# Second head's keys loaded by quarters, x tiles 10 and 11 loaded later, half of a tile's statistics moved: a fused LayerNorm, attention and gated FFN kernel

## The chip, the core and the metric

The kernel runs on one core of a Trainium2 chip. The core has a matrix engine (TensorE, PE in the profile, with its weight loads listed as PEld), a vector engine (DVE), a scalar engine (ACT), GpSimd (POOL) and a sync engine (SP) that does nothing here but issue DMAs. The metric is the device time of one execution in microseconds.

## The reference

```python
xn = layernorm(x)                                   # x: 2048 x 640, bf16
q  = (xn @ wq) as 32 heads of 192
s  = softmax(q @ k_cache.T * 192**-0.5) @ v_cache   # 2048 keys per head, not causal
s  = s.reshape(2048, 32 * 192) @ wo
h  = silu(xn @ w1) * (xn @ w3)                      # F = 1536
g  = silu(h @ w2)
out = x + s * g
```

Keys and values come from a cache, so only the queries are projected here. Rows of x are normalised over their 640 columns, without scale or bias.

## The kernel before

The 2048 rows of x are 16 tiles of 128 rows, and four tiles make a block of 512 queries. Each of the 32 heads is worked in four passes, one for each block. A pass has eight steps p = 0 to 7. Step p takes the two key tiles p and p + 8 (128 keys each): `scores` (L506) makes six matmuls into one of the two buffers of tile `st2`, `weights` (L513) takes the exponential on ACT and writes `pT2`, and `values` (L546) makes 16 matmuls that add to the two output banks `obank0` and `obank1`. The value matmuls run about a step behind the scores. At the end of a pass `evict` (L522) reads each bank on DVE into `osum`, and the next pass can write a bank only when it has been read.

A head of 192 columns doesn't fit 128 partitions, so the keys, turned by the DMA, lie in three tiles: `KA` has columns 0 to 127 of all 2048 keys, `KB` columns 64 to 191, and `KC` is put together from them by POOL (L154, L155), for the first two heads in two halves. `KC` copy 0 takes keys 1024 to 1535 of `KA` and keys 0 to 511 of `KB`; copy 1 takes keys 1536 to 2047 and 512 to 1023. Steps 0 to 3 of a pass therefore read keys 0 to 511 and 1024 to 1535, and steps 4 to 7 the others.

From the third head on everything is loaded far ahead. The first two heads are different: there the program starts, and x has to be loaded, normalised and turned while the first passes are running already. The passes of the first two heads are interleaved as in `order` (head, block): (0, 0), (1, 0), (0, 1), (0, 2) and so on; they are numbered n = 0, 1, 2, ... The rest is written out by hand. `posts` names what is put behind step p of pass n, and `extras` what is put into it. Nearly all of these calls are pinned, so each engine runs them in the order in which the program calls them:

- `load_x(engine, t0, t1)` (L194) loads tiles t0 to t1 - 1 of x.
- `ln_stats(i)` makes the statistics of tile i on DVE: two `bn_stats` of 320 columns and one `bn_aggr` (L237, L238).
- `ln_root(i0, n)` makes 1 / sqrt(var + eps) of n tiles on ACT, a logarithm (L244) and an exponential (L247).
- `scale_and_turn(i)` normalises tile i on DVE (L255, tile `xn`) and turns it into `xnT` with a DMA from SP (L266).
- `late_project(h, qb)` projects the queries of a block (L348). In pass 1, step 5 it does head 0, block 1, which reads the turned tiles 4 and 5 in the first half of its matmuls, and 6 and 7 in the second.
- `next_bound` (L443, L446, L449) makes the bound that stands for the row maximum in the exponentials of a pass. For pass 1 it needs `KC` copy 0 of head 1 (`first_key_maxima`, L415 and L424).

SP's queue is run in program order as well. Ahead of the change it holds, after the keys of the first head: values 0 (first half), x tiles 4 and 5, `KA` of head 1, values 0 (second half), `KB` of head 1, x tiles 6 and 7, values 1 (first half), x tiles 8 and 9, values 1 (second half), x tiles 10 and 11, then the turned tiles 4 to 7, x tiles 12 to 15, and the turned tiles 8 to 11. In the program as built, each of these DMAs also waits for the DMA eight places ahead of it to have landed, since eight semaphores are used in turn.

After the 32 heads come the output projection, the FFN's second product and the stores (L865, L889). They aren't touched.

Of the kernel before, what the change touches and what calls it, by code (L numbers as in the profile page):

```python
# [11 lines left out]
BF16 = mybir.dt.bfloat16  # L12
F32 = mybir.dt.float32
I32 = mybir.dt.int32

P = 128
# [14 lines left out]
def _kernel_impl(ctx, tc, A_x, A_k_cache, A_v_cache, A_wq, A_wo, B_w1, B_w3, B_w2, out):  # L31
    nc = tc.nc
    _, SQ, D = A_x.shape
    _, H, SK, dh = A_k_cache.shape
# [8 lines left out]
    HALF = SK // 2  # L43
# [22 lines left out]
    pin = tc.keep_in_program_order  # L66
# [31 lines left out]
    kvp = kvstack.enter_context(tc.tile_pool(name="kvp", bufs=3))  # L98
# [23 lines left out]
    def load_key_part(h, s, half, k0, k1, keep):  # L122
        d0 = (0, DH - P)[s]
        return keep(nc.sync.dma_start_transpose(out=half[:, k0:k1], in_=A_k_cache[0, h][k0:k1, d0:d0 + P]))  # L124

    def load_key_half(h, s, keep):
        half = kvp.tile([P, SK], BF16, tag=("KA", "KB")[s], name=("KA", "KB")[s])
        load_key_part(h, s, half, 0, SK, keep)
        return half
# [9 lines left out]
    def load_values_part(h, vt, r0, r1):  # L139
        of = A_v_cache[0, h].rearrange("(t r p) d -> p t r d", t=2, p=P)  # L140
        to = vt[:].rearrange("p (t r) d -> p t r d", t=2)
        for t in range(2):
            pin(nc.sync.dma_start(out=to[:, t, r0:r1, 0:DH], in_=of[:, t, r0:r1, :]))  # L143
# [33 lines left out]
    with ExitStack() as actx:  # L177
# [6 lines left out]
        lnp = lctx.enter_context(tc.tile_pool(name="lnp", bufs=2, side="right"))  # L184
# [4 lines left out]
        nsub = 2  # L189
        mv = lnx.tile([P, NQT, nc.vector.BN_AGGR_DIM], F32, name="mv")  # L190
        x_all = lnx.tile([P, NQT, D], BF16, name="x_all")

        def load_x(eng, t0, t1):
            pin(eng.dma_start(out=x_all[:, t0:t1, :], in_=x2[t0 * P:t1 * P, :].rearrange("(t p) d -> p t d", p=P)))  # L194
# [35 lines left out]
                                      reason="not all at once")  # L230
                    behind = None

        def ln_stats(i):
            st6 = lnp.tile([P, nsub, nc.vector.BN_STATS_DIM], F32, tag="st6", name="st6")
            xr = x_all[:, i, :].rearrange("p (a f) -> p a f", a=nsub)
            for a in range(nsub):
                pin(nc.vector.bn_stats(out=st6[:, a, :], in_=xr[:, a, :]))  # L237
            return pin(nc.vector.bn_aggr(out=mv[:, i, :], in_=st6[:]))  # L238

        rstd = {}  # L240

# [45 lines left out]
        squares = stats_on_scalar(1)  # L287
        squares()
        keys0 = second_keys(ln_stats(0))
        values0 = kvp.tile([P, NKT, DH + 2], BF16, tag="vt", name="vt")  # L290
        load_values_part(0, values0, 0, 4)
        load_x(nc.sync, 4, 6)
        KA1 = load_key_half(1, 0, pin)
        load_values_part(0, values0, 4, 8)
        keys1 = KA1, load_key_half(1, 1, pin)
        load_x(nc.sync, 6, 8)
        values1 = kvp.tile([P, NKT, DH + 2], BF16, tag="vt", name="vt")
        load_values_part(1, values1, 0, 4)
        load_x(nc.sync, 8, 10)
        load_values_part(1, values1, 4, 8)  # L300
        load_x(nc.sync, 10, 12)

        keep_busy(2, behind=ln_stats(2))
        ln_root(0)
        keep_busy(1, behind=ln_stats(3))
        ln_root(2)
        for i in range(4):
            ln_scale(i)
        turned = []
        for i in range(4):  # L310
            pool, tag = (ps_st, "st2") if i < 2 else (ps_o, f"ob{3 - i}")
# [360 lines left out]
        for h in range(2):  # L672
# [14 lines left out]
        }  # L687
        posts = {
            (0, 0): ((complete_second,),),
            (0, 2): ((ln_root, 4), (scale_and_turn, 4), (scale_and_turn, 5), (first_key_maxima, 1)),  # L690
            (0, 3): ((next_bound, 1, 0), (lambda: loads.pop("second half")(),)),
            (0, 5): ((ln_stats, 6), (ln_stats, 7)),
            (1, 0): ((ln_root, 6),),
            (1, 1): ((scale_and_turn, 6), (scale_and_turn, 7), (load_x, nc.sync, 12, 16)),
            (1, 2): ((ln_stats, 8), (ln_stats, 9)),
            (1, 3): ((ln_stats, 10), (ln_stats, 11)),
            (1, 5): ((scale_and_turn, 8), (scale_and_turn, 9), (scale_and_turn, 10), (scale_and_turn, 11)),
            (2, 2): ((ln_stats, 12), (ln_stats, 13)),
# [340 lines left out]
@with_exitstack  # L1039
def kernel(  # L1040
    ctx: ExitStack,
    tc: tile.TileContext,
    A_x: bass.AP,
    A_k_cache: bass.AP,
    A_v_cache: bass.AP,
    A_wq: bass.AP,
    A_wo: bass.AP,
    B_x: bass.AP,
    B_w1: bass.AP,
    B_w3: bass.AP,  # L1050
    B_w2: bass.AP,
    out: bass.AP,
):
    _kernel_impl(ctx, tc, A_x, A_k_cache, A_v_cache, A_wq, A_wo, B_w1, B_w3, B_w2, out)
# [30 lines left out]
```

## Time and profile before

| what | us |
|---|---|
| median of 3 runs | 1936.01 |
| lowest and highest of them | 1935.34, 1936.47 |
| the profiled execution | 1934.81 |
| its span, first to last instruction | 1933.0 |
| PE busy in the span | 1926.7 |
| ACT busy | 1278.1 |
| DVE busy | 1029.6 |
| POOL busy | 414.5 |

All times of rows below count from the start of the span. A row of the timeline gives start, duration, engine, line of the kernel, operation, output and input, and how many instructions of the kind are merged into it; in square brackets stands the idle time of the engine ahead of it and who ended it. "SPq" is SP's queue: the duration is that of issuing, and the landing of the data is told in another view, counted from the start of issuing. The granted clock of TensorE was 1.000 in the whole span.

### The profile page before, as it was taken

What the parts mean: (1) busy time and instruction counts of PE and PEld (TensorE: products, weight loads), DVE (VectorE), ACT (ScalarE), POOL (GpSimd) and SP (SyncE); (2) the same over time, 40 slices, a digit from 0 to 9 for tenths busy, and PEclk for the clock granted to TensorE, in tenths of its full rate; (3) what the DMA queues carried; (4) which work ended last, traced back from release to release, by engine and by line L of the source; (5) the groups of instructions that cost most, each with busy time, mean ns of one, the idle gap of its engine ahead of it and who ended that gap; (6) DMA issues with size and microseconds to landing.
All of it is one profiled execution on the core that took longest, in us unless ns stands there. A gap on an engine that the chain in (4) does not pass through costs nothing.

```text
span 1933.0 us, 60455 instructions
## 1 busy us (share of the span) xinstructions
PE 1926.7 (100%) x27269; PEld 1411.1 (73%) x27269; DVE 1029.6 (53%) x1892; ACT 1278.1 (66%) x1296; POOL 414.5 (21%) x637
## 2 busy tenths in 40 slices
PE   9999999999999999999999999999999999999999
PEld 6789899998777766666666666666666666577776
DVE  7775555565656565656565555555565554521111
ACT  7777777777777777777777777777777777210000
POOL 2432222222222222222222222222222110000000
PEclk9999999999999999999999999999999999999999
DMA  8532323232213232233432232323232102937873
GB/s 181 105 77 55 77 47 85 47 85 43 65 45 68 51 68 57 63 82 77 109 63 69 55 77 55 76 47 85 47 85 45 36 8 76 281 67 137 156 153 57
DMA packets 361672, 152.84 MB, mean 79 GB/s; under 512 B 312544, under 2 KB 355232, under 8 KB 361408
## 3 DMA queue, kind: packets, MB, share of 16 engines
q1 hardware_dynamic: 346832, 120.12, 29.5%
q0 software_dynamic: 7872, 23.60, 4.7%
q10 hardware_dynamic: 6704, 5.21, 1.0%
q8 instruction: 214, 3.51, 0.7%
q14 instruction: 50, 0.41, 0.1%
HBM read 56.23 MB, written 31.98 MB: 46 GB/s over the span
## 4 chain that ended last, share of the span: by engine, by line
PE 98%; DVE 1%; SPq 1%; DMA 0%; issue 0%; ACT 0%
PE st L506 35%; PE obank L546 34%; PE ps L348 14%; PE ps_s L865 11%; PE ps_f L889 3%; PE ps_gu L332 1%; PE ps_gu L348 0%; SPq L124 0%; DMA x_all<-in_A_x_dram 0%; DVE osum L522 0%; DVE st L237 0%; SPq L143 0%; DVE st L415 0%; DVE pa L487 0%; DVE ostage L529 0%; DVE qF L393 0%
## 5 line engine op out<-in xcount | busy, mean ns | idle before, releaser
L513 ACT ACTIVATE pT<-st,nb 128x1024 bf16<-128x1024 f32 x960 | 1068.4, 1113 | 326.6 <-PE st L506 322.2
L546 PEld LDWEIGHTS <-pT 64*128 64x128 bf16 x16384 | 754.3, 94 | 201.4 <-issue 1.7
L546 PE MATMUL obank<-vt,pT 64*128 64x193 bf16 x16384 | 872.7, 243 | 0.4 <-DVE osum L522 0.4
L522 DVE TENSOR_REDUCE osum<-obank 128x386 f32<-128x772 f32 x256 | 234.2, 956 | 580.2 <-PE obank L546 580.1
L506 PE MATMUL st<-qA,KA 64*128 64x512 bf16 x2048 | 409.8, 376 | 0.1
L506 PE MATMUL st<-qS,KB 64*128 64x512 bf16 x1024 | 385.1, 376 | 0.0
L506 PE MATMUL st<-qS,KC 64*128 64x512 bf16 x1024 | 384.9, 376 | 0.0
L506 PE MATMUL st<-qD,KC 64*128 64x512 bf16 x960 | 361.2, 376 | 0.0
L506 PE MATMUL st<-qF,KB 64*128 64x512 bf16 x960 | 361.0, 376 | 0.0
L348 PE MATMUL ps<-xnT,w 64*128 64x512 bf16 (+1 forms) x2540 | 318.7, 374 | 0.0
L382 POOL COPY qS<-qA 64x512 bf16<-64x512 bf16 x254 | 161.7, 637 | 616.3 <-ACT qA L392 609.2
L506 PEld LDWEIGHTS <-KC 64*128 64x128 bf16 x2048 | 192.4, 94 | 99.8
L348 PEld LDWEIGHTS <-w 64*128 64x128 bf16 x2540 | 146.7, 94 | 96.9
L865 PE MATMUL ps_s<-wo_sb,oT 128*128 128x320 bf16 (+2 forms) x1536 | 208.8, 299 | 0.0
L506 PEld LDWEIGHTS <-KB 64*128 64x128 bf16 x2048 | 192.4, 94 | 5.5
L865 PEld LDWEIGHTS <-oT 128*128 128x128 bf16 x1536 | 148.2, 98 | 60.6
L529 DVE TENSOR_TENSOR ostage<-osum,rl_all 128x384 bf16<-128x384 f32 x256 | 155.4, 607 | 8.8
L506 PEld LDWEIGHTS <-KA 64*128 64x128 bf16 x2048 | 127.4, 93 | 15.4 <-issue 1.4
L108 POOL DMA_DIRECT2D w<-in_A_wq_dram x60 | 52.9, 882 | 289.1 <-PE ps L348 288.9
L393 DVE CAST qF<-ps 128x512 bf16<-128x512 f32 x120 | 82.9, 690 | 52.2 <-ACT qA L392 52.2
L870 DVE SCALAR_TENSOR_TENSOR tmp<-ps_s,g_all 128x320 f32<-128x320 f32 (+2 forms) x32 | 15.6, 487 | 176.1 <-PE ps_s L865 176.1
L376 DVE TENSOR_REDUCE st<-qA 128x1 f32<-128x512 bf16 (+1 forms) x130 | 87.3, 672 | 4.2 <-ACT qA L392 4.1
(101 smaller groups left out, 1131.4 us busy)
## 6 DMA issues: line engine op xcount, KB each, us to landing
o_scr<-ostage SPq DMA_DIRECT2D x64, 384.0 KB, 2.7
vt<-in_A_v_cache_dram SPq DMA_DIRECT2D x30, 768.0 KB, 6.1
wo_sb<-in_A_wo_dram POOLq DMA_DIRECT2D x1, 7680.0 KB, 32.6
w<-in_A_wq_dram POOLq DMA_DIRECT2D x30, 160.0 KB, 3.4
hT_scr<-hblk SPq DMA_DIRECT2D x16, 256.0 KB, 3.0
xt<-in_A_x_dram POOLq DMA_DIRECT2D x16, 160.0 KB, 8.7
w<-in_B_w_dram POOLq DMA_DIRECT2D x30, 80.0 KB, 2.6
w<-in_A_wq_dram POOLq DMA_DIRECT2D x30, 80.0 KB, 2.8
```

Of the source, the lines that this page charges most:

```text
L108: return lambda eng: keep(eng.dma_start(out=w[:, :, c0:c1], in_=src[:, s0:s0 + c1 - c0].rearrange("(c p) d -> p c d", p=P)))
L348: mm = pin(nc.tensor.matmul(out[:, t * 512 + t0 * P:t * 512 + (t0 + step) * P], lhsT=ws[t][ROWS[r], c, :], rhs=rows_of(qb, c, ROWS[r], t0, ...
L376: pin(nc.vector.tensor_reduce(out=hd["st"][r, 2 + s, qb:qb + 1], in_=src[r, qb * 512:qb * 512 + n], axis=AX.X, op=ALU.max, apply_absolute_ ...
L382: return [lambda t=t: keep(copy(out=hd["qS"][ROWS[t], qs], in_=hd["qA"][ROWS[1 - t], qs])) for t in range(2)]
L393: pin(cast(out=hd["qF"][:, qs], in_=ps[:, 512:1024]))
L506: pin(nc.tensor.matmul(st2[:, t * 512:(t + 1) * 512], lhsT=keys, rhs=q[ROWS[t], qs], start=(s == 0), stop=(s == 2)))
L513: pin(nc.scalar.activation(out=pT2[:, c0:c1], in_=st2[:, c0:c1], func=ACT.Exp, scale=SCALE, bias=nb))
L522: pin(nc.vector.tensor_reduce(out=osum[:], in_=ob[:].rearrange("p t (j c) -> p j c t", j=2)[:, :, 0:DH + 1, :], axis=AX.X, op=ALU.add))
L529: pin(nc.vector.tensor_tensor(out=ostage[:, b * 2:b * 2 + 2, hg * DH:(hg + 1) * DH], in0=osum[:, :, 0:DH], in1=rl.unsqueeze(2).to_broadcas ...
L546: pin(nc.tensor.matmul(acc["o"][b][:, r, j * 256:j * 256 + DH + 1], lhsT=pT2[ROWS[r], t * 512 + i * P:t * 512 + (i + 1) * P], rhs=vt[ROWS[ ...
L865: pin(nc.tensor.matmul(ps, lhsT=oT[:, k, :], rhs=wo_sb[:, k, c0:c1], start=(k == 0), stop=(k == OC - 1)))
L889: pin(nc.tensor.matmul(ps[:, pi * 512:pi * 512 + c1 - c0], lhsT=hT[:, fc, qsl], rhs=w2_sb[:, fc, c0:c1], start=(fc == 0), stop=(fc == FC - ...
```

## The change

The two transposing loads of the second head's keys, of 2048 keys each, become eight of 512 keys. The four for steps 0 to 3 stand where `KA` and `KB` were loaded; the four for steps 4 to 7 stand behind the load of x tiles 8 and 9 and ahead of the second half of values 1. The load of x tiles 10 and 11 goes from the end of that list to behind the turning of tiles 4 and 5. `ln_stats` can do one half of a tile: the second `bn_stats` of tile 7 and its `bn_aggr` go from pass 0, step 5, to pass 1, step 1, which lies behind the evictions of pass 0 on DVE. `ln_root(6)` goes from behind step 0 of pass 1 to behind step 1, and the two `bn_stats` of tile 8 go from step 2 to step 1, one on each side of the scaling of tiles 6 and 7.

```diff
-        def ln_stats(i):
-            st6 = lnp.tile([P, nsub, nc.vector.BN_STATS_DIM], F32, tag="st6", name="st6")
+        half_stats = {}
+
+        def ln_stats(i, a0=0, a1=nsub):
+            if a0 == 0:
+                half_stats[i] = lnp.tile([P, nsub, nc.vector.BN_STATS_DIM], F32, tag="st6", name="st6")
             xr = x_all[:, i, :].rearrange("p (a f) -> p a f", a=nsub)
-            for a in range(nsub):
-                pin(nc.vector.bn_stats(out=st6[:, a, :], in_=xr[:, a, :]))
-            return pin(nc.vector.bn_aggr(out=mv[:, i, :], in_=st6[:]))
+            for a in range(a0, a1):
+                pin(nc.vector.bn_stats(out=half_stats[i][:, a, :], in_=xr[:, a, :]))
+            if a1 == nsub:
+                return pin(nc.vector.bn_aggr(out=mv[:, i, :], in_=half_stats.pop(i)[:]))
...
         load_x(nc.sync, 4, 6)
-        KA1 = load_key_half(1, 0, pin)
+        keys1 = [kvp.tile([P, SK], BF16, tag=tag, name=tag) for tag in ("KA", "KB")]
+
+        def second_head_keys(s, k0, k1):
+            for t0 in (0, HALF):
+                load_key_part(1, s, keys1[s], t0 + k0, t0 + k1, pin)
+
+        second_head_keys(0, 0, HALF // 2)
         load_values_part(0, values0, 4, 8)
-        keys1 = KA1, load_key_half(1, 1, pin)
+        second_head_keys(1, 0, HALF // 2)
         load_x(nc.sync, 6, 8)
         values1 = kvp.tile([P, NKT, DH + 2], BF16, tag="vt", name="vt")
         load_values_part(1, values1, 0, 4)
         load_x(nc.sync, 8, 10)
+        second_head_keys(0, HALF // 2, HALF)
+        second_head_keys(1, HALF // 2, HALF)
         load_values_part(1, values1, 4, 8)
-        load_x(nc.sync, 10, 12)
...
-            (0, 2): ((ln_root, 4), (scale_and_turn, 4), (scale_and_turn, 5), (first_key_maxima, 1)),
+            (0, 2): ((ln_root, 4), (scale_and_turn, 4), (scale_and_turn, 5), (load_x, nc.sync, 10, 12),
+                     (first_key_maxima, 1)),
             (0, 3): ((next_bound, 1, 0), (lambda: loads.pop("second half")(),)),
-            (0, 5): ((ln_stats, 6), (ln_stats, 7)),
-            (1, 0): ((ln_root, 6),),
-            (1, 1): ((scale_and_turn, 6), (scale_and_turn, 7), (load_x, nc.sync, 12, 16)),
-            (1, 2): ((ln_stats, 8), (ln_stats, 9)),
+            (0, 5): ((ln_stats, 6), (ln_stats, 7, 0, 1)),
+            (1, 1): ((ln_stats, 7, 1, 2), (ln_root, 6), (ln_stats, 8, 0, 1), (scale_and_turn, 6), (scale_and_turn, 7),
+                     (ln_stats, 8, 1, 2), (load_x, nc.sync, 12, 16)),
+            (1, 2): ((ln_stats, 9),),
```

## The prediction

> **What bounds the kernel now.** I read the page first, for the engine that fills the span; then PE's waits; then the chain that ended last, in order of time, where it isn't PE; then PE, DVE, ACT and SP one by one between 11 and 37 us, which is all that the change moves.
>
> ```profile
> PE 1926.7 (100%) x27269; PEld 1411.1 (73%) x27269; DVE 1029.6 (53%) x1892; ACT 1278.1 (66%) x1296; POOL 414.5 (21%) x637
> ```
>
> The reader is to see that PE is busy for 1926.7 of 1933.0 us, so all idle time of PE in the kernel is 6.3 us. The waits of PE, of the first 200 us:
>
> ```profile
> PE fill L226 <- DVE mv L238: 1.5, 2, 1.1
> PE fill L226 <- PEq L1069: 0.8, 1, 0.8
> PE obank L546 <- DVE osum L522: 0.4, 1, 0.4
> ```
>
> Two of the three lie in the first 7 us, before any score, and aren't touched. What the change can take away is the third. The chain in order of time tells what stands behind it (start, duration, what):
>
> ```profile
> 11.64 3.44 SPq L124
> ...
> 16.29 3.44 SPq L124
> ...
> 19.78 3.52 DMA x_all<-in_A_x_dram
> ...
> 23.32 0.90 DVE st L237 x2
> ...
> 24.45 0.76 DVE st L237 x2
> ...
> 25.23 0.21 DVE mv L238
> 25.44 1.71 DVE osum L522 x2
> ...
> 27.19 0.84 PE obank L546 x16
> 28.03 0.65 PE st L506 x6
> 28.68 0.67 PE obank L546 x16
> ```
>
> This is the path into the steady part: SP is held by the keys of the second head (two times 3.44 us), so x tiles 6 and 7 are issued only at 19.78 and land at 23.30; their statistics fill DVE to 25.44, the two evictions of pass 0 come behind them, and PE waits. From 27.19 on the chain is PE without a break: a step is 0.65 for six scores and 0.67 for 16 value matmuls (0.042 each).
>
> The gap on PE itself:
>
> ```profile
> 25.28 0.50 PE L546 MATMUL obank<-vt,pT 64*128 64x193 bf16 x8
> ...
> 26.32 0.51 PE L546 MATMUL obank<-vt,pT 64*128 64x193 bf16 x8
> 27.19 0.84 PE L546 MATMUL obank<-vt,pT 64*128 64x193 bf16 x16 [0.36 <-DVE osum L522]
> 27.86 0.40 PE L506 MATMUL st<-qA,KA 64*128 64x512 bf16 x2
> ...
> 29.17 0.40 PE L506 MATMUL st<-qA,KA 64*128 64x512 bf16 x2
> ```
>
> Pass 0 ends at 25.78. Eight matmuls from 26.32 should take 8 x 0.042 = 0.34, to 26.65; the next begins at 27.19. So PE loses 0.54 us here, and no more than that is to be had: 0.03% of the time. What is left is whether something else turns late.
>
> **The change part by part.** The sum is made against the profiled execution, 1934.81 us (span 1933.0 and 1.81 around it); the median of the runs is 1.20 higher, and the difference found is added to the median.
>
> *The statistics of tile 7.* DVE and ACT before:
>
> ```profile
> 26.19 0.95 DVE L522 TENSOR_REDUCE osum<-obank 128x386 f32<-128x772 f32 x1
> 27.05 0.44 DVE L255 TENSOR_SCALAR xn<-x_all,mv,rstd 128x640 bf16<-128x640 bf16 x1
> ```
>
> ```profile
> 25.48 0.29 ACT L244 ACTIVATE lv<-mv,eps_t 128x2 f32<-128x2 f32 x1 [0.28 <-DVE mv L238]
> 25.80 0.20 ACT L247 ACTIVATE rstd<-lv 128x2 f32<-128x2 f32 x1
> 25.91 2.10 ACT L513 ACTIVATE pT<-st,nb_all 128x1024 bf16<-128x1024 f32 x2
> ...
> 33.59 1.11 ACT L513 ACTIVATE pT<-st,nb_all 128x1024 bf16<-128x1024 f32 x1 [0.64 <-PE st L506]
> ```
>
> Without the second half and the aggregate (0.4 + 0.2 us) DVE is free at about 24.8 even if x tiles 6 and 7 land no earlier, since tile 6 and half of tile 7 take 23.32 to 24.8. The first eviction then goes with PE's last matmul into bank 0; the second can't begin before 25.78, and with 0.05 of latency runs 25.83 to 26.78 (0.95). PE goes on 0.04 later, as at 27.15 to 27.19, so at 26.82: 0.37 us sooner than before. Tile 7's second half now stands behind the evictions: `bn_stats` to 27.13, aggregate to 27.36. `ln_root(6)` waits for it on ACT, 27.40 to 27.92 by its rows. Behind it on ACT stands the exponential of step 2, which began at about 26.96 before (the second of two in 2.10) and now ends at 27.92 + 1.05 = 28.97. Its score buffer is the one that step 4 writes, so PE's scores at 29.17 can come at 29.0 at the earliest, though PE itself would be there at 27.86 - 0.37 + 1.31 = 28.80. Of 0.37 us gained, 0.17 are left.
>
> *The scaling of tiles 6 and 7* began at 27.05 and 27.41, each 0.44 long. It now waits for `ln_root(6)`: 27.97 and 28.33. The `bn_stats` of tile 8 put in front fits into the time in which DVE waits for ACT and costs nothing; if tile 8 landed after 27.9 (27.0 before) it would hold the scaling. SP, with its landings:
>
> ```profile
> 28.12 1.23 SPq L266 DMA_TRANSPOSE xnT<-xn  x1
> ```
>
> ```profile
> 29.44 1.23 SPq L266 DMA_TRANSPOSE xnT<-xn  x1
> ```
>
> ```profile
> xnT<-xn SPq DMA_TRANSPOSE x1, 2.7
> ```
>
> ```profile
> 31.63 1.27 PE L348 MATMUL ps<-xnT,w 64*128 64x256 bf16 x20
> 32.72 0.40 PE L506 MATMUL st<-qA,KA 64*128 64x512 bf16 x2
> ```
>
> Before, tile 7 was issued at 29.44 and landed at 32.14; the projection needs it in the middle of its 1.09 us, at 32.17. There is no slack. After, tile 6 is issued when its scaling has ended, at 28.44, tile 7 1.31 behind (28.12 to 29.43 above, say 29.75), and it lands at 32.45. PE, 0.17 ahead, would be there at 32.0 and waits 0.45. Net: +0.28 us. Tile 6's own landing took
>
> ```profile
> xnT<-xn SPq DMA_TRANSPOSE x1, 3.0
> ```
>
> and with that for tile 7 too it is +0.6; with the 3.8 that is the median of loads of x below, +1.4. The other end is -0.17, should the data land 0.45 sooner.
>
> *Keys by quarters.* Two transposes become eight; SP executes six more instructions. By the rows:
>
> ```profile
> 8.41 1.46 SPq L124 DMA_TRANSPOSE KB<-in_A_k_cache_dram  x1
> ```
>
> ```profile
> KB<-in_A_k_cache_dram SPq DMA_TRANSPOSE x1, 5.4
> ```
>
> 1024 keys took 1.46 to issue, 2048 took 3.44 (11.64 and 16.29): 512 keys lie between 0.73 (half of 1.46) and 1.23 (a turned tile of 640 columns). I take 0.9, nearer to the keys' own rows: eight are 7.2 against 6.88, +0.3 on SP; the ends are -1.0 and +3.0. SP reached the turning of tile 4 at 23.72 with the load of x 10 and 11 in front, 0.64 with its gap; it now gets there at about 23.1 + 0.3. That hides the cost. On the other side x tiles 6 and 7 are issued two quarters of each key tile earlier, 3.4 us, so at about 16.4, and `KC` copy 0 and the bound of pass 1 come earlier by as much. PE didn't wait for these, so it is worth nothing.
>
> The late quarters go behind x 8 and 9. All that lies in front of values 1, second half, is the same as before, and that landed 5.8 after its issue:
>
> ```profile
> vt<-in_A_v_cache_dram SPq DMA_DIRECT2D x1, 192.0 KB, 5.8
> ```
>
> ```profile
> 24.54 0.61 POOL L154 COPY KC<-KA 64x512 bf16<-64x512 bf16 x1
> ```
>
> It was issued at 22.53, so it landed at 28.3; with the queues drained in order the late keys land ahead of it, by about the 1.3 us that it takes, at 27. Two POOL copies (0.61 each) bring `KC` to 28.2, if they begin with the landing. The scores of step 4 need it at 29.0. Cover: 0.8 us. If the keys land by more than that later, PE waits for all of the rest.
>
> *x tiles 10 and 11* were issued at 23.08 and landed
>
> ```profile
> x_all<-in_A_x_dram SPq DMA_DIRECT2D x1, 320.0 KB, 6.2
> ```
>
> later, at 29.3. They now go behind tile 5. Tile 6 was issued at 28.12 behind tile 5 and the load; without the load's 0.64 and with the 0.3 of the quarters that place comes at 27.8, and less 0.6 (the queue is emptier by this load, a guess) I take 27.2. All loads of x landed after
>
> ```profile
> DMA to landing us min/median/max: 2.7/3.8/6.2
> ```
>
> so at 29.9 to 33.4, with the median at 31.0. Statistics of two tiles took 23.32 to 25.44, 2.12; `ln_root(8, 4)` 0.52. So it ends at 33.64, and ACT's next exponential, at 33.59 before and at 33.87 with the +0.28, has it covered by 0.2. The worst landing ends it at 36.0: 2.4 us late.
>
> The sum: -0.37 (gap) + 0.20 (exponential behind the root) + 0.45 (tile 7) + 0 + 0 = +0.28 us. From 1934.81 that is 1935.1, and from the median **1936.3 us**.
>
> A page speaks against the change. The Trainium skill, "DMA: Bandwidth & Descriptors", section "Anatomy of one DMA — SWDGE (gpsimd) path", gives every DMA a fixed cost of about 2.0 us besides its bytes, mostly the receipt of the last write. It is written of another issuing path than SP's; if it were paid in series here, six more DMAs would be an estimated 12 us, and the time 1948. The trace disagrees on "in series": tiles 6 and 7 were issued 1.32 us apart with landings of 3.0 and 2.7. What a series would do here is the last rival below, from rows.
>
> **The rivals.**
>
> *The gain goes through* (tile 7 and the root in time): the score buffer alone gives -0.17, nothing late gives -0.37, and the whole gap -0.54: 1935.5 to 1935.8. For it: SP reaches tiles 4 and 5 earlier, so the data engines may be less loaded when 6 and 7 go. Against: scaling 6 is bound by a chain on DVE and ACT that the change makes 0.9 longer.
>
> *x tiles 10 and 11 late*: +0.8 to +2.4, 1936.8 to 1938.4. For it: the same load took 6.2 before. Against: the queue is emptier behind the turned tiles; between 28 and 29 us the data engines were at a share of 0.34:
>
> ```profile
> 28.00:29.00 1.00, 1.00 (x20) 0.72 (x16) 0.96 (x4) 0.29 (x2) 0.00 (x0) 1.00 0.34 41
> ```
>
>
> *The split doesn't free SP*: the quarters issue at 1.23 each, 9.8 us instead of 6.9, and x tiles 6 and 7 gain 1.9 instead of 3.4. Nothing of the sum rests on their being early, so 1936.3 stays; only the late quarters and what follows move, by up to 3.0 - 0.8 of cover: 1938.2 at the end.
>
> *Slower*: the late quarters land in series, each with a landing of its own between 3.0 (a turned tile) and 5.4 (all of `KB`). They are issued from about 18.5 on, 2.1 behind x 6 and 7 as x 8 and 9 follow them. Four in a row land at 30.5 to 40.1; at the middle of 4.2, at 35.3, and PE's step 4, due at 29.0, stops for 6.3 us: 1942.3. It decides from a landing at 32.9 on, 3.9 us (0.2%) behind step 4, or 3.6 us for each. Against: in the rows above transposes overlap.
>
> **How the numbers follow.** 0.2% is 3.9 us, about what a measurement of this kernel can tell from no change. Forecast 0.50; gain through 0.25; x 10 and 11 late 0.15; split without freeing SP 0.06; late quarters in series 0.03; something that I don't see that gains as much, 0.01, though PE's idle time after the first 7 us can't give it. All but the last two lie within 0.2%. The range from 1935.3 to 1937.8 takes in the whole gain and most of the late loads, with the runs' own spread of 1.1; it leaves out about 0.15.
>
> **What would show it.** Right: PE's second bank of pass 1 at 26.8 in place of 27.19; ACT's root at 27.4, directly ahead of an exponential; turned tile 7 issued at about 29.75; PE's projection at 31.5 with an idle stretch in its middle, and the next scores at 33.0 in place of 32.72. Wrong: a wait of PE or POOL for `KA` or `KB` near 29, DVE idle before the statistics of tile 10 past 31.5, or SP idle while it waits for a landing ahead of the late quarters.

## The result, and the profile after

The changed kernel takes 1942.24 us (median of 7 runs, 1939.59 to 1943.44); the kernel before, beside it, 1935.56 (1935.17 to 1936.57). The ratio is 1.0029, with a 95% interval from 1.0019 to 1.0039. So it is slower, by 3.7 to 7.5 us, where 0.3 us had been forecast. The profiled execution took 1940.08 us, with a span of 1938.2: 5.27 us more than the one before. It is the second shortest of the seven; by the medians the loss is 6.7 us, so about 1.4 us of it don't stand in this trace.

Lines of the new profile are those of the changed kernel: the turned tiles are at L270, the projection at L359, the scores at L517, the value matmuls at L557.

The waits of PE, whole span (engine, line, waited for: us in total, times, longest):

```profile
PE ps L359 <- DMA xnT<-xn: 2.9, 2, 1.7
PE fill L226 <- DVE mv L242: 0.9, 2, 0.5
PE fill L226 <- PEq L1081: 0.8, 1, 0.8
PE obank L557 <- ACT pT L524: 0.4, 1, 0.4
```

The wait for the evictions is gone. Two others stand in its place: one of 0.4 for an exponential, and two, 2.9 us together, of the projection for turned tiles. SP's queue tells why they are late (start, duration of issuing, what):

```profile
11.54 2.45 SPq L124 DMA_TRANSPOSE KA<-in_A_k_cache_dram  x2
14.04 1.13 SPq L143 DMA_DIRECT2D vt<-in_A_v_cache_dram  x2
15.21 3.13 SPq L124 DMA_TRANSPOSE KB<-in_A_k_cache_dram  x2
18.39 0.58 SPq L194 DMA_DIRECT2D x_all<-in_A_x_dram  x1
...
20.63 2.46 SPq L124 DMA_TRANSPOSE KA<-in_A_k_cache_dram  x2
23.13 3.46 SPq L124 DMA_TRANSPOSE KB<-in_A_k_cache_dram  x2
...
27.88 2.56 SPq L270 DMA_TRANSPOSE xnT<-xn  x2
30.50 0.57 SPq L194 DMA_DIRECT2D x_all<-in_A_x_dram  x1
31.16 3.10 SPq L270 DMA_TRANSPOSE xnT<-xn  x2
```

The eight quarters hold the queue for 2.45 + 3.13 + 2.46 + 3.46 = 11.50 us, where two whole transposes took 6.88. The turning of tile 4 is issued at 27.88 in place of 23.72. PE around it (a row in brackets: idle time ahead of it, and who ended it):

```profile
27.49 0.40 PE L517 MATMUL st<-qA,KA 64*128 64x512 bf16 x2
...
29.04 0.51 PE L557 MATMUL obank<-vt,pT 64*128 64x193 bf16 x8 [0.39 <-ACT pT L524]
29.38 0.38 PE L517 MATMUL st<-qA,KA 64*128 64x512 bf16 x2
...
33.78 0.72 PE L359 MATMUL ps<-xnT,w 64*128 64x256 bf16 x10 [1.71 <-DMA xnT<-xn]
35.70 1.24 PE L359 MATMUL ps<-xnT,w 64*128 64x256 bf16 x10 [1.20 <-DMA xnT<-xn]
36.73 0.64 PE L517 MATMUL st<-qA,KA 64*128 64x512 bf16 x2
```

The first ten matmuls of the projection take 0.72 us, the second ten 1.24, and two matmuls of scores 0.64 in place of 0.40. The reason is in the granted clock of TensorE, in stretches of 1 us (columns: us, PE busy and instructions, granted clock, share of the data engines, GB/s):

```profile
32.00:33.00 1.00, 0.07 (x2) 1.00 0.76 223
33.00:34.00 1.00, 0.22 (x5) 1.00 1.52 202
34.00:35.00 1.00, 0.50 (x10) 1.00 0.91 181
35.00:36.00 1.00, 0.30 (x4) 0.87 0.36 53
36.00:37.00 1.00, 1.00 (x12) 0.50 0.68 212
37.00:38.00 1.00, 1.00 (x6) 0.50 1.03 376
38.00:39.00 1.00, 1.00 (x12) 0.50 0.24 62
39.00:40.00 1.00, 1.00 (x23) 0.93 0.68 132
```

PE is busy for 0.07, 0.22, 0.50 and 0.30 of four stretches, then the clock is halved for 0.26 + 3 + 0.14 = 3.4 us (a mean of 0.87 is 0.26 us at half). Nothing like it stands in the profile before, where it is 1.00 throughout.

The 5.27 us can be followed on PE, by the difference of like rows in the two traces. The scores of step 3 of pass 1 come 0.37 earlier (27.49 against 27.86), those of step 4 0.21 later (29.38 against 29.17). The projection starts at 33.78 instead of 31.63 + 0.21: 1.94 more. Its second half is due 0.54 behind that, at 34.32, and starts at 35.70: 1.38 more. The scores behind it start at 36.73 in place of 32.72, 4.01 later in all, so the half clock has cost 0.48 by then, and it costs about 1.2 more until 40 us (the next scores are at 40.50 in place of 35.30, 5.20 later). That makes 0.21 + 1.94 + 1.38 + 1.7 = 5.2.

### The profile page after: what moved, and what is told of

It reads as the page before. It is cut to its first block, busy times and chain, and to the rows that moved or that the text cites. A ratio compares the mean times of both kernels' runs of the same rounds, so it can differ in the third digit from the quotient of the medians.

```text
span 1938.2 us, 60461 instructions
## 1 busy us (share of the span) xinstructions
PE 1929.4 (100%) x27269; PEld 1419.0 (73%) x27269; DVE 1028.7 (53%) x1892; ACT 1278.2 (66%) x1296; POOL 414.4 (21%) x637
## 4 chain that ended last, share of the span: by engine, by line
PE 98%; DVE 1%; DMA 0%; SPq 0%; ACT 0%; issue 0%
PE st L517 35%; PE obank L557 34%; PE ps L359 14%; PE ps_s L877 11%; PE ps_f L901 3%; PE ps_gu L343 1%; PE ps_gu L359 0%; DVE osum L533 0%; DMA x_all<-in_A_x_dram 0%; SPq L270 0%; DMA xnT<-xn 0%; DVE st L240 0%; DVE st L426 0%; PE pst L266 0%; DVE pa L498 0%; DVE ostage L540 0%
## 5 line engine op out<-in xcount | busy, mean ns | idle before, releaser
L557 PEld LDWEIGHTS <-pT 64*128 64x128 bf16 x16384 | 758.3, 94 | 197.7 <-issue 1.2
L557 PE MATMUL obank<-vt,pT 64*128 64x193 bf16 x16384 | 875.3, 243 | 0.5 <-ACT pT L524 0.4
L517 PE MATMUL st<-qA,KA 64*128 64x512 bf16 x2048 | 412.4, 376 | 0.1
L517 PE MATMUL st<-qS,KC 64*128 64x512 bf16 x1024 | 385.2, 376 | 0.0
L517 PE MATMUL st<-qS,KB 64*128 64x512 bf16 x1024 | 385.1, 376 | 0.0
L517 PE MATMUL st<-qF,KB 64*128 64x512 bf16 x960 | 361.0, 376 | 0.0
L517 PE MATMUL st<-qD,KC 64*128 64x512 bf16 x960 | 361.0, 376 | 0.0
L359 PE MATMUL ps<-xnT,w 64*128 64x512 bf16 (+1 forms) x2540 | 320.5, 375 | 2.9 <-DMA xnT<-xn 2.9
L517 PEld LDWEIGHTS <-KC 64*128 64x128 bf16 x2048 | 192.3, 94 | 97.8 <-issue 0.3
L359 PEld LDWEIGHTS <-w 64*128 64x128 bf16 x2540 | 148.8, 94 | 99.5 <-issue 2.5
L517 PEld LDWEIGHTS <-KB 64*128 64x128 bf16 x2048 | 192.4, 94 | 6.4
L517 PEld LDWEIGHTS <-KA 64*128 64x128 bf16 x2048 | 128.7, 93 | 15.5 <-issue 1.4
```

The costliest lines, as they stand in the source:

```text
L359: mm = pin(nc.tensor.matmul(out[:, t * 512 + t0 * P:t * 512 + (t0 + step) * P], lhsT=ws[t][ROWS[r], c, :], rhs=rows_of(qb, c, ROWS[r], t0, ...
L517: pin(nc.tensor.matmul(st2[:, t * 512:(t + 1) * 512], lhsT=keys, rhs=q[ROWS[t], qs], start=(s == 0), stop=(s == 2)))
L557: pin(nc.tensor.matmul(acc["o"][b][:, r, j * 256:j * 256 + DH + 1], lhsT=pT2[ROWS[r], t * 512 + i * P:t * 512 + (i + 1) * P], rhs=vt[ROWS[ ...
```

## The experiments

Three theories were to be told apart. S: the split costs issuing; a transpose holds SP's queue for a time that hardly depends on its size, so everything behind the quarters is late. O: the new order costs, whatever the number of transposes. D: the moved statistics cost. Beside them stood the question what the clock adds.

### The parts one by one

**unsplit**: the keys whole again in their old places, the other moves kept.

```diff
-        second_head_keys(0, 0, HALF // 2)
+        KA1 = load_key_half(1, 0, pin)
         load_values_part(0, values0, 4, 8)
-        second_head_keys(1, 0, HALF // 2)
+        keys1 = KA1, load_key_half(1, 1, pin)
...
-        second_head_keys(0, HALF // 2, HALF)
-        second_head_keys(1, HALF // 2, HALF)
```

> The changed kernel with the second head's keys loaded whole again, in two transposes where they stood before; x tiles 10 and 11 and the half of tile 7's statistics stay moved. Theory S (the split costs issuing: a transpose of 512 keys holds SP's queue for 1.2 us or more, so the turned tiles come 4 us late): SP reaches the turning of tile 4 at about 23.1, PE has no wait for turned tiles above 0.7 us, and the time is 1935.0 to 1936.4, as before. Rival O (the new order costs, with x tiles 10 and 11 between the turned tiles): DVE waits over 1 us for x, and the time is over 1937. Rival D (the moved statistics and root hold ACT and the scaling): over 1936.5.

Measured: 1936.93 (10 runs) against 1936.85 (30 runs), ratio 1.0004 (0.9994 to 1.0013). With the split the loss is gone, within this interval of -1.2 to +2.5 us; the kernel before is itself slower in this group than the times of the expectation suppose, so the ratio is what counts. DVE waits 0.5 us for x tile 10, under the 1 us of O. In its profile tile 4 is issued at 23.43, but PE still waits 1.3 us for turned tiles, more than the 0.7 that S allowed:

```profile
PE ps L351 <- DMA xnT<-xn: 1.3, 1, 1.3
```

Tiles 6 and 7 were issued at 28.81 and 30.11 there, near the 28.44 and 29.75 of the prediction, and then took this long to land:

```profile
xnT<-xn SPq DMA_TRANSPOSE x1, 4.8
```

```profile
xnT<-xn SPq DMA_TRANSPOSE x1, 4.0
```

They took 3.0 and 2.7 before. The load of x tiles 10 and 11 now goes directly in front of them.

**stats_only**: the kernel before, with the statistics and the root moved, and nothing else.

```diff
...
-            (0, 5): ((ln_stats, 6), (ln_stats, 7)),
-            (1, 0): ((ln_root, 6),),
-            (1, 1): ((scale_and_turn, 6), (scale_and_turn, 7), (load_x, nc.sync, 12, 16)),
-            (1, 2): ((ln_stats, 8), (ln_stats, 9)),
+            (0, 5): ((ln_stats, 6), (ln_stats, 7, 0, 1)),
+            (1, 1): ((ln_stats, 7, 1, 2), (ln_root, 6), (ln_stats, 8, 0, 1), (scale_and_turn, 6), (scale_and_turn, 7),
+                     (ln_stats, 8, 1, 2), (load_x, nc.sync, 12, 16)),
+            (1, 2): ((ln_stats, 9),),
```

> The kernel before with only the statistics and the root moved (tile 7's second half, its root, tile 8's first half). The prediction's own terms: -0.37 for the gap, +0.20 for the exponential behind the root, +0.45 for turned tile 7: 0.28 slower than before, between -0.4 and +0.6. Rival D: 1 us slower or more, with PE's wait for turned tiles as after. Theory S says nothing but that it is near the kernel before.

Measured: 1937.05 (10 runs) against 1936.85, ratio 1.0004 (0.9994 to 1.0013). Its profile has no wait for turned tiles; tiles 6 and 7 land in 2.9 and 2.6. So theory D falls, by the trace: the times alone would allow 2.5 us. What the profile has is the wait for the exponential behind the root:

```profile
29.55 0.51 PE L550 MATMUL obank<-vt,pT 64*128 64x193 bf16 x8 [0.39 <-ACT pT L517]
```

So this wait belongs to the moved root. Unsplit differs from this kernel only in the moved load of x, which makes that load a suspect for its longer landings; but this is one trace of each, and two runs below speak against it.

**keys_only**: the changed kernel without the moves of the statistics and of x tiles 10 and 11.

```diff
...
         load_values_part(1, values1, 4, 8)
+        load_x(nc.sync, 10, 12)
...
-            (0, 2): ((ln_root, 4), (scale_and_turn, 4), (scale_and_turn, 5), (load_x, nc.sync, 10, 12),
-                     (first_key_maxima, 1)),
+            (0, 2): ((ln_root, 4), (scale_and_turn, 4), (scale_and_turn, 5), (first_key_maxima, 1)),
...
```

> The changed kernel without the moves of x tiles 10 and 11 and of the statistics: only the keys by quarters, late ones behind x tiles 8 and 9. Theory S: SP needs some 4 to 5 us more for eight key transposes than for two, reaches the turning of tile 4 at 28 to 29 (23.72 before), PE waits 2 to 4 us for turned tiles, and the time is 1939.5 to 1944. Rival O, with the late x tiles 10 and 11 as the cause: under 1937.5, since that load is back in front.

Measured: 1940.50 (9 runs) against 1936.85, ratio 1.0019 (1.0009 to 1.0029). The keys alone bring the loss, with x tiles 10 and 11 back in front. From its profile, the turning of tiles 4 to 7 on SP, and PE's wait:

```profile
28.75 5.72 SPq L266 DMA_TRANSPOSE xnT<-xn  x4
```

```profile
PE ps L356 <- DMA xnT<-xn: 3.1, 2, 2.7
```

Its clock is at half for 3.4 us behind this wait (means of 0.62, 0.50, 0.50 and 0.67 in the four stretches of 1 us from 36 on: 0.76 + 2 + 0.66).

### The split by itself

**split_in_place**: the kernel before, with each of the two transposes cut into four in its old place.

```diff
-        KA1 = load_key_half(1, 0, pin)
+        keys1 = [kvp.tile([P, SK], BF16, tag=tag, name=tag) for tag in ("KA", "KB")]
+
+        def second_head_keys(s):
+            for k0 in range(0, SK, 512):
+                load_key_part(1, s, keys1[s], k0, k0 + 512, pin)
+
+        second_head_keys(0)
         load_values_part(0, values0, 4, 8)
-        keys1 = KA1, load_key_half(1, 1, pin)
+        second_head_keys(1)
```

> The kernel before with the two key transposes of the second head each cut into four of 512 keys, in the same places; nothing else moved. Theory S: SP needs 4 to 5 us more, x tiles 6 and 7 and all that follows are issued 4 to 5 us later, PE waits for KC, for evictions behind the statistics or for turned tiles, and the time is 3 to 7 us longer than before. Rival O: no more than 1 us longer.

Measured: 1940.62 (10 runs) against 1936.80 (27 runs), ratio 1.0018 (1.0009 to 1.0027). The order is the old one, and the loss is there all the same. SP:

```profile
13.19 5.99 SPq L124 DMA_TRANSPOSE KA<-in_A_k_cache_dram  x4
...
20.39 5.09 SPq L124 DMA_TRANSPOSE KB<-in_A_k_cache_dram  x4
```

That is 11.1 us in place of 6.88. PE's waits are others, since the delay now strikes the loads ahead of the turned tiles; the clock is 1.00 around them:

```profile
PE obank L552 <- DVE osum L528: 2.6, 2, 2.3
...
PE obank L552 <- DMA vt<-in_A_v_cache_dram: 0.9, 1, 0.9
PE st L512 <- DMA KB<-in_A_k_cache_dram: 0.8, 1, 0.8
```

**sizes**: the kernel before, with the keys of three later heads cut, where the queue has little else to do.

```diff
-        ks = load_keys(h, free)
+        if h in (8, 12, 16):
+            n = {8: 512, 12: 1024, 16: 256}[h]
+            ks = [kvp.tile([P, SK], BF16, tag=tag, name=tag) for tag in ("KA", "KB")]
+            for s in range(2):
+                for k0 in range(0, SK, n):
+                    load_key_part(h, s, ks[s], k0, k0 + n, free)
+        else:
+            ks = load_keys(h, free)
```

> The kernel before with the keys of heads 8, 12 and 16 loaded by 512, by 1024 and by 256 keys in place of 2048, in the steady part where the queue has little else. What one transpose holds SP's queue: theory S, a floor of about 1.2 us whatever the size up to 640 columns (512 and 256 keys alike 1.15 to 1.25, 1024 about 1.4, 2048 about 2.2). Rival, proportional to the keys as the prediction had it: 256 about 0.4, 512 about 0.8.

Measured, as the rows of SP's queue, for 512, 1024 and 256 keys at a time:

```profile
322.50 5.49 SPq L124 DMA_TRANSPOSE KA<-in_A_k_cache_dram  x4
328.10 5.11 SPq L124 DMA_TRANSPOSE KB<-in_A_k_cache_dram  x4
...
525.41 2.52 SPq L124 DMA_TRANSPOSE KA<-in_A_k_cache_dram  x2
...
728.26 11.84 SPq L124 DMA_TRANSPOSE KA<-in_A_k_cache_dram  x8
```

Within such groups the medians of one were 1.24 us for 256 keys, 1.25 for 512, and 1.23 and 1.30 for 1024; single ones took up to 2.03. So, by the medians, a transpose holds SP for about 1.25 us whatever its size from 256 to 1024 keys. The 2048 keys of a whole load cost 1.3 to 3.5 us in the same run, between 370 and 680 us; what adds to the floor there isn't shown. The kernel as a whole took 1935.62 in its only run: there the time on SP is hidden.

**halves**: the order of the changed kernel with four transposes of 1024 keys. For the second head, the columns of `KA` and `KB` are counted so that the keys of steps 0 to 3 are one run, and `KC` and the values are loaded to match; the result of attention doesn't depend on the order of the keys.

```diff
...
         def second_head_keys(s, k0, k1):
-            for t0 in (0, HALF):
-                load_key_part(1, s, keys1[s], t0 + k0, t0 + k1, pin)
+            load_key_part(1, s, keys1[s], 2 * k0, 2 * k1, pin)
...
+            if hd["h"] == 1:
+                l0 = (p // 4) * HALF + (p % 4) * P
+                lo, hi = slice(l0, l0 + P), slice(l0 + 512, l0 + 512 + P)
...
```

> The changed kernel with the same order of loads, but four transposes of 1024 keys in place of eight of 512: the columns of KA and KB of the second head are counted so that the keys of steps 0 to 3 are one run of 1024, and its values are loaded to match. Theory S (each transpose of 512 keys or fewer holds the queue for about 1.2 us, one of 1024 for 1.4 to 1.6): the four take about 6 to 6.5 us on SP in place of 11.5, the turning of tile 4 is issued at 22.5 to 24, PE's wait for turned tiles falls from 2.9 to under 1.5 us, the clock stays at 1.00, and the time is that of the kernel before, within 1.5 us. Rival O (late keys ahead of the turned tiles cost by their order): SP and PE stay as in the changed kernel, 3 us or more slower than before.

**after_again**: the changed kernel itself, on the chip of halves.

> The changed kernel itself, beside the others of this call: 3 to 7 us slower than before; two waits of PE for turned tiles and a granted clock of about 0.5 for some 3 us behind them.

Measured, against 1936.80: halves 1938.27 (11 runs), ratio 1.0011 (1.0002 to 1.0020); the changed kernel 1940.76 (10 runs), ratio 1.0022 (1.0013 to 1.0032). The halves win back 2.5 us by the medians, a part and not all of it; the two intervals overlap. The profiled execution of halves, at 1936.98, is the shortest of its runs. SP's rows:

```profile
11.62 1.52 SPq L124 DMA_TRANSPOSE KA<-in_A_k_cache_dram  x1
...
14.36 3.11 SPq L124 DMA_TRANSPOSE KB<-in_A_k_cache_dram  x1
...
19.74 1.28 SPq L124 DMA_TRANSPOSE KA<-in_A_k_cache_dram  x1
21.06 2.37 SPq L124 DMA_TRANSPOSE KB<-in_A_k_cache_dram  x1
```

They take 8.3 us, not the 6 to 6.5 expected: each `KB` half took longer than the floor. So tile 4 is issued at 25.48 (22.5 to 24 expected), and PE waits 1.7 us (under 1.5 expected). The clock stays at 1.00. Tiles 6 and 7 land after 4.9 and 4.2 us, as in unsplit. In its profile here the changed kernel waits 3.6 us, with its clock at half from 36.6 to 40.

**halves_x_back**: the same with the load of x tiles 10 and 11 directly behind that of 8 and 9.

```diff
...
         load_x(nc.sync, 8, 10)
+        load_x(nc.sync, 10, 12)
...
```

> The kernel with four transposes of 1024 keys, and the load of x tiles 10 and 11 put right behind that of 8 and 9 rather than between the turned tiles 5 and 6. If a load of x directly in front of turned tiles 6 and 7 makes them land later (4.9 and 4.2 us in the halves run, 3.0 and 2.7 before): they land in about 3 us, PE's wait for them falls from 1.7 to under 0.8, and the time is within 1 us of before. If not: a wait of 1.3 to 2 as in the halves run, 1 to 2 us slower than before.

Measured: 1937.55 (11 runs) against 1936.82 (31 runs), ratio 1.0005 (0.9996 to 1.0014). The time is near before, as expected if the load of x was the cause, but the wait is not, so the reason isn't shown. In the profiled execution, which at 1939.20 was one of the longer runs, the second `KB` half held the queue for 4.22 us, tile 4 was issued at 28.69, tiles 6 and 7 took 4.3 and 3.8 to land, and PE waited 2.0 for them, with the clock at 1.00, and 0.5 for the late `KC`. So the landings of tiles 6 and 7 aren't set by a load of x in front alone; what else makes them long, and why `KB` takes up to 4.2 us, stays open.

### The clock

**filler**: the changed kernel, with 14 matmuls on constants in PE's wait.

```diff
             def part(ph):
+                if step == 2 and ph == 0:
+                    for _ in range(14):
+                        pin(nc.tensor.matmul(out[:, 0:256], lhsT=one_l, rhs=one_r[:, 0:256], start=True, stop=True))
```

> The changed kernel with 14 extra matmuls of 256 columns on constants put ahead of the projection of head 0's second block, into the bank that the projection then starts anew; they fill 1.5 us of PE's wait for the turned tiles. If part of the loss is the clock that falls after the wait: the turned tiles land as in the changed kernel (PE's projection halves at 33.8 and 35.7), but the granted clock stays 1.00 from 35 to 40 us, the time is 1938 to 1939, and the runs lie closer together than 1939.6 to 1943.4. If the clock fell for another reason: 1940 to 1943 as the changed kernel.

Measured: 1939.39 (10 runs, 1938.63 to 1941.67) against 1936.85, ratio 1.0016 (1.0006 to 1.0025): just above the 1938 to 1939 expected for the clock. To compare with the changed kernel on one chip, both were run again.

> The changed kernel, for the pair with the filler on one chip: 4 to 7 us slower than before, clock at half for about 3 us behind the waits, runs spread over 4 us or more.

> The filler kernel once more, beside the changed kernel on one chip. If the clock is part of the loss: 1 to 3 us faster than the changed kernel, at the same landings of the turned tiles, clock 1.00 throughout. If the waits are the whole loss: within 0.5 us of the changed kernel.

Measured, against 1936.82 (31 runs): the changed kernel 1941.46 (11 runs, 1938.97 to 1943.78), ratio 1.0023 (1.0014 to 1.0032); with the filler 1939.45 (11 runs, 1939.06 to 1942.89), ratio 1.0017 (1.0008 to 1.0026). The medians are 2.0 us apart; the intervals overlap. The traces are clear. With the filler (filler_pair) the halves of the projection start at 34.26 and 36.64, with a wait of 1.7 us, and the clock is 1.00:

```profile
35.00:36.00 1.00, 0.00 (x0) 1.00 0.96 190
36.00:37.00 1.00, 0.36 (x8) 1.00 0.44 40
37.00:38.00 1.00, 1.00 (x16) 1.00 0.66 197
```

In the changed kernel beside it the first half doesn't wait, at 32.35, and the second starts earlier than with the filler:

```profile
36.45 0.72 PE L359 MATMUL ps<-xnT,w 64*128 64x256 bf16 x10 [3.38 <-DMA xnT<-xn]
```

But there the clock is halved for about 3.4 us (means of 0.92, 0.50, 0.50, 0.50 and 0.87 in the five stretches of 1 us from 37 on: 0.16 + 3 + 0.26). So the filler wins nothing but the clock. The spread hardly narrowed: 7 of 11 runs with the filler lie within 0.6 us of each other, one is at 1942.89.

**gap**: the kernel before, with PE held back by a matmul that reads x tile 12.

```diff
...
+            if (h, qb) == (0, 1):
+                pin(nc.tensor.matmul(ps[:, 0:128], lhsT=one_l, rhs=x_all[:, 12, 0:128], start=True, stop=True))
             first()
```

> The kernel before with one more matmul ahead of the projection of head 0's second block, that reads x tile 12 and so holds PE until x tiles 12 to 15 have landed at about 36.5 instead of 31.6: an idle stretch of PE of 4 to 5 us with nothing split or moved. If idle PE time makes the clock fall: granted clock 0.5 for about 3 us behind it, and the time 5.5 to 8 us longer than before, over the wait itself. If the clock in the changed kernel fell for its DMA traffic: clock 1.00, the time longer by the wait alone, 4 to 5 us.

Measured: 1942.20 (8 runs) against 1936.82, ratio 1.0027 (1.0017 to 1.0038). That is 5.4 us by the medians, between the two ranges expected, and the interval of 3.3 to 7.4 us reaches into both, so the trace has to decide. It has a wait of 4.8, and the clock at half for the same 3.4 us (means of 0.96, 0.50, 0.50, 0.50 and 0.83 in the stretches from 36 on: 0.08 + 3 + 0.34). PE's rows around it:

```profile
37.02 0.29 PE L366 MATMUL ps<-x_all,const-bfloat16-1.0 128*128 128x128 bf16 x1 [4.80 <-DMA x_all<-in_A_x_dram]
37.25 2.31 PE L348 MATMUL ps<-xnT,w 64*128 64x256 bf16 x20
```

Nothing is split or moved here. The idle time of PE is enough to halve the clock.

This profile also bears on the landings. SP's queue is that of the kernel before, and tiles 6 and 7, issued at 28.86 and 30.18, yet took 4.6 and 4.1 us to land, against 3.0 and 2.7 before and 2.9 and 2.6 in stats_only. The same order thus gives short and long landings in different executions.

## Why the prediction was wrong

The gap was read rightly. PE came 0.37 us earlier at 27.49, as worked out, and it was the bound: no more than 0.54 was to be had. What failed is the price on the other side.

*Keys by quarters: the step that failed.* The prediction took 0.9 us for a quarter, "nearer to the keys' own rows", and +0.3 on SP for all. Measured: 1.44 each in the changed kernel, 1.25 as a floor in the run with other sizes, +4.6 in all. The right row was in the prediction and was used as an upper end only: a turned tile of 640 columns took 1.23, 1024 keys 1.46. Two sizes with nearly the same price were read as a slope through zero; they were a floor. Even the upper end, +3.0, was too low, because the quarters of `KB` took up to 2.15. At this price x tiles 6 and 7 were issued only 1.4 us earlier (18.39), not 3.4.

*What is late behind them.* The prediction said of this end that "only the late quarters and what follows move", and set 0.8 us of cover against it, the cover of `KC`. But what follows was the turning of tiles 4 to 7, of which the same text says that there is no slack at 32.17. A delay on SP reaches them nearly whole: tile 4 was issued 4.2 us later, tile 7 3.6 later (33.04), and it landed 3.5 later (35.64 against 32.14); PE paid 1.94 and 1.38. The late quarters themselves nearly held: `KC` came from POOL in time for all but some hundredths of a microsecond of step 4, with 0.2 us of waiting in keys_only and 0.5 in halves_x_back.

*The clock.* It was no term of the sum, and 1.7 of the 5.2 us are it. The Trainium skill, "TensorE: Matmul & The Clock Gate", section "Part 1: The HAM clock gate (the "warmup" mystery)", says that TensorE falls to half its clock after an idle window of about 3.4 us and needs as long a busy one to come back. The traces agree on the second: in the changed kernel, keys_only and gap the half clock lasted 3.4 us each. On the first they show that no single idle stretch of that length is needed: 1.71 and 1.20 with ten matmuls between them did it, in the four stretches shown above. Waits of 2.0 us in halves_x_back and of 2.3 and 0.4 in split_in_place left it at 1.00. An estimate of the runs' spread follows from it: a mean clock of 0.999 was shown by runs of 1939.6 to 1941.1, and 0.998 by those of 1942.2 to 1943.4, so the longer runs have more half-clock time, by about one more such window; no trace of one was taken.

*The statistics of tile 7.* The term was +0.20 for the exponential behind the root; the changed kernel lost 0.58 there (from 0.37 ahead to 0.21 behind). The value matmuls that use the exponential had to wait for it; the prediction had looked at the score buffer alone. In stats_only the whole came out within the noise.

*Scaling of tiles 6 and 7.* The term was +0.45 from a landing of 2.7. Two kernels have it without the split: in stats_only PE didn't wait at all, in unsplit it waited 1.3, with a landing of 4.0. The prediction had 3.8 as an end, at +1.4. What makes a landing short or long stays open.

*x tiles 10 and 11* were later than the rival had it: issued at 30.50 in place of 27.2, and landed at 34.4, behind its worst of 33.4. DVE waited for them, which the prediction had listed as a sign of being wrong.

```profile
34.43 0.89 DVE L240 BATCH_NORM_STATS2 st<-x_all 128x6 f32<-128x320 bf16 x2 [3.69 <-DMA x_all<-in_A_x_dram]
```

ACT then waited 3.87 us for the root. That lies beside PE's own wait for turned tiles, and no wait of PE in the list above goes back to it. In keys_only, with the load back in front, DVE still waits 2.5 us for these tiles and ACT 1.5 for the root, since SP is late there too; the loss is nearly the same.

*The rivals.* "The split doesn't free SP" was the right mechanism, with the wrong place for its price. "Late quarters in series" was right on the sign alone: its 1942.3 us is the measured median by luck, since PE never stopped 6.3 us for the keys. "About what can be told" was set at 0.2%, and the result lies just above it.

## What to carry to other kernels

Before a transfer is cut, look for a floor in the price of issuing it: two rows of different sizes with nearly the same time point to one, and then the number of instructions is what counts, at least 1.25 us or so for each transposing DMA here. What an issue queue loses is paid by whatever stands behind it with the least slack, so find that first. And where waits of TensorE close together added up to 2.9 us or more, as in the changed kernel, keys_only and gap, some 3.4 us at half clock came on top, here a loss of 1.7 us.

## What had not been expected of the hardware

The time of issuing one DMA transpose on SP was 1.24 us for 256 keys, 1.25 for 512, and 1.23 and 1.30 for 1024, by the medians, while a plain load of x of 320 KB took 0.51 to 0.58 in the kernel before. The granted clock fell to 0.50 for 3.4 us after idle time that was broken by ten matmuls. And landings of turned tiles 6 and 7 ranged from 2.6 to 4.9 us, with long ones also where SP's queue was that of the kernel before.
